# A linear-attention and feed-forward kernel: the second unit's output projection by seven block products, its weight sums in parts and one step sooner

## The chip, the cores and the metric

The kernel runs on one core of a Trainium2 chip. The metric is the device time of one execution in microseconds (us). A core has five engines with queues of their own: TensorE (PE; PEld is its weight load), VectorE (DVE), ScalarE (ACT), GpSimd (POOL) and SyncE (SP, which here only issues transfers). Each engine takes its instructions in the order of its queue; they wait for each other through semaphores.

## The reference

```python
# attention: r, k, v, w of (4, 8, 768, 48), u of (8, 48); state (4, 8, 48, 48) from zero
for t in range(768):
    cur = outer(u * k[t], v[t])
    y[t] = r[t] @ (state + cur)
    state = w[t][:, None] * state + outer(k[t], v[t])
x = y as (3072, 384)             # tokens by heads times head size
h = x @ w_in                     # w_in (384, 2048)
g = h * erf(softplus(h))
out = g @ w_out                  # w_out (2048, 384)
```

All is 32-bit floating point.

## The kernel before

The 3072 tokens are handled in 12 units of 256 tokens (two batches of 128 tokens each, called j). Step s of the kernel does the attention of unit s, and beside it pieces of the feed-forward block of earlier units: the hidden layer of unit s-1 (`hidden`, L1098: six matmuls of 256 columns to a tile `ff`, three to one accumulator half) and the output projection of unit s-3 (`project` or `project_fast`). The order is written out by hand: the attention code calls `place(n)` at eight places of a step (`run(n, ...)` from step 5 on), and a place emits pieces from lists of letters. P is a piece of projection, H a piece of the hidden layer, A the next activation stage of a unit, S1 to S4 are sums of activations, G a sum of weights. The schedule of an engine is the order of emission; nothing reorders it.

Attention. A step splits its 128-token chunks into halves of 64 and combines them by levels 1 to 6. At each level TensorE makes the products (`level_products`, L628), VectorE scales r and k in place for the next level (`scale`, L334; level n+1's products need level n's scaling), and VectorE takes the products of the levels up to 5 under a mask into `own` (`take_level`, L638; ScalarE, L645, takes level 6). From step 5 on, the first levels are done in another way, by rows: VectorE and GpSimd multiply and fade r and k (L456, L463, L485 to L504, L535, L538), VectorE sums the terms (L529), and the sums go out to memory and come back in another order (`by_blocks`, `by_tokens`) to be written into `own` (L590). That work for step s+1 is a generator, `following`, that the step s before it moves on by `next(following)`; each `yield` in `prepare` is where it pauses. In step 4 (`DIRECT`), which makes levels 4 to 6 by itself, it is moved on after level 4, after level 5 and after level 6. The state goes on through `middle` (L1032), a fading on GpSimd (L1018 and L1035) and the state sum (L1036).

Activation. For units 0 to 2, ScalarE makes softplus and erf of half a unit (2048 columns) in `room`, four quarters of 1024 columns, two of them for each half of the unit; VectorE multiplies the result into `h` in two instructions (L1087). `STAGES` and the letter A say how many of these stages are emitted where.

Projection. `project` (L1130) multiplies h by w_out plainly: 32 matmuls of 384 columns for a unit, in two accumulators, and ScalarE copies each out (L1139). `project_fast` (L1213) splits the unit's h in four blocks (a11, a12, a21, a22: by tokens and by halves of the 2048) and w_out in four (b11 to b22), and makes the four output blocks from seven block products of eight matmuls of 192 columns. It needs sums of activations, s1 to s4 (`blend`, L1190 to L1196; s1, s2 and s4 lie in quarters 1, 2 and 3 of `room`, s3 in place of a21), and sums of weights, t1 to t4 (`mix_weights`, L1154; t2, t3 and t4 lie in `mixed`, t1 in place of b12). It uses two accumulators, m0 and m1, which come from the same pool of two buffers as those of the hidden pieces. The sixth and the seventh product are added to the output by VectorE (L1233, L1238), and only then is m0, and m1, free for the next piece. [...]

`SEVEN = 2` says that units 0 and 1 are projected plainly and the others by seven products. Unit 0 is projected in step 3, places 0 to 3; unit 1 in step 4:

```python
order = (
    "A P P P", "A P P P", "A P P H H", "A A S1 S2 G H H s H", "ep H s H m S4 S3 ep H",
)
```

The weight sums t3, t2, t4 are made by VectorE near the end of step 3 (three sums of 1536 columns), t1 by GpSimd in step 4 (G), after the last plain product of unit 1 has read b12. Until the start of step 3, w_out is still being put together from 64-bit words (L261 to L289): its last three pairs of row tiles become ready at places 0 to 2 of step 3.

Of the kernel before, what the change touches and what calls it, by code (L numbers as in the profile page):

```python
# [15 lines left out]
ALU = mybir.AluOpType  # L16

P = 128
FAST = 3
SEVEN = 2  # L20
EP = 64
HC = 64
NC = 2
NJ = 2
FG = 8
# [15 lines left out]
DIRECT = 4  # L41
NEAR_LOG = 4
NEAR = 1 << NEAR_LOG
LOG = 6
# [18 lines left out]
def kernel(  # L63
# [14 lines left out]
    nc = tc.nc  # L78
    PSUM = bass.MemoryType.PSUM

    n_steps, _, _, JP, C = rkw.shape
# [4 lines left out]
    _, NT, DM = w_out.shape  # L86
# [31 lines left out]
    first = const.tile([P, HC], FP32, name="first")  # L118
# [241 lines left out]
    def prepare(s):  # L360
# [185 lines left out]
            add_total(beside, 2)  # L546
        fade(nc.vector, r, 2)
        sum_up(0)
        multiply(nc.vector, 3)
        if levels == NEAR_LOG:  # L550
            fade(beside, k, 3)
# [397 lines left out]
    def attend(s, xT, early, place, behind):  # L949

        c, in_t, vt, made, S, S_next, ends = parts_of(s)
        K = in_t[:, 1]
        RK = by_pair(in_t)


        following = prepare(s + 1) if s + 1 < n_steps else iter(())
        own = made if s >= DIRECT else att.tile([P, NH, HC], FP32, name="own")

        if s == DIRECT:
            next(following)  # L960
        for level in range(near_log(s) + 1 if s == DIRECT else 1, LOG + 1):
            rk = by_pair(made) if level == 1 else RK
            pp = turns.pop("pp", None) or products([P, NE, JP, HC])
            if s == level == 1:
                level_products(pp, rk, level, range(NP))
                turns.pop("hop")()
                level_products(pp, rk, level, range(NP, JP))
                send("br")
            elif s != 2 or level != 2:
                level_products(pp, rk, level)  # L970
            if level == LOG and s == DIRECT:
                spread_blocks(s + 1, pp)
            if s == 1 and 2 < level:
                stages["h"](level + 1)
            scale(s, level)
            if s == 1 and level == 2:
                turns.pop("pending")()
            if s == 1 and level < 3:
                stages["h"](level + 1)
            if s == 1 and level > 1:  # L980
                nc.gpsimd.tensor_copy(out=block_sb[:, 0:1], in_=K[:, 0, 0:1])
                for i in {2: (2, 3)}.get(level, (level + 1,)):
                    stages["o"](i)
            if s != 1:
                early(level - 1)
            got = pp[:].rearrange("p e n t -> p (e n) t")
            if level == 1:
                nc.vector.tensor_mul(
                    own[:], got, first[:, None, :].to_broadcast([P, NH, HC])
                )  # L990
            else:
                take_level(own, pp, level)
            if level > 1 and (s, level) != (1, 4):
                next(following, None)
            if s == 2 and level == 1:

                def ahead():
                    turns["pp"] = products([P, NE, JP, HC])
                    level_products(turns["pp"], RK, 2)

                turns["ahead"] = ahead
            place(level - 1)
            if (s, level) == (1, 4):
                next(following, None)
            if s == 1 and level in (3, 4):
                nc.sync.dma_start(out=loaded[2][0][:, level - 3], in_=rkw[2][:, level - 3])

        from_own(s, own, 1)
        ps = products([P, JP, P])
        for n in range(JP):  # L1010
            nc.tensor.transpose(ps[:, n, :], K[:, n, :], ident[:])  # L1011
        kT = att.tile([P, NH, D], FP32, name="kT", bufs=1)
        nc.scalar.copy(
            kT[:].rearrange("p (e n) d -> p e n d", e=NE),
            ps[:].rearrange("p n (e d) -> p e n d", e=NE)[..., :D],
        )
        if c:
            nc.gpsimd.tensor_mul(  # L1018
                faded[0][:], S[:], ends[:, :, 0:1].to_broadcast([P, JP, D])
            )  # L1020
        next(following, None)
        place(LOG)
        if s == DIRECT - 1:
            for _ in range(3):
                mixing.send(nc.vector)

        ps = products([P, NC, JP, HC])
        ps = [[ps[:, h]] * NE for h in range(NC)]
        state_part(s, kT, ps)
        from_own(s, own, 0)  # L1030
        if c:
            nc.vector.tensor_add(middle[both], faded[0][both], ps[0][0][both, :, :D])  # L1032
        else:
            nc.vector.tensor_copy(middle[both], ps[0][0][both, :, :D])
        nc.gpsimd.tensor_mul(faded[1][:], middle[:], ends[:, :, 1:2].to_broadcast([P, JP, D]))  # L1035
        nc.vector.tensor_add(S_next[both], faded[1][both], ps[1][0][both, :, :D])  # L1036
        for _ in following:
            pass
        place(LOG + 1)
        through_state(s, xT)  # L1040
        behind()
# [102 lines left out]
    def mix_weights():  # L1144

        upper, lower = w_out_sb[:, :FG], w_out_sb[:, FG:]
        b11, b12, b21, b22 = (x[:, :, k * ND : (k + 1) * ND] for x in (upper, lower) for k in range(2))
        t3, t2, t4 = (mixed[:, n] for n in range(3))
        for of, a, op, b in (
            (t3, b22, ALU.subtract, b12), (t2, t3, ALU.add, b11),  # L1150
            (t4, b21, ALU.subtract, t2), (b12, b12, ALU.subtract, b11),
        ):
            engine = yield
            engine.tensor_tensor(out=of, in0=a, in1=b, op=op)  # L1154
        yield

    def half_room(name, shape):
        t = wide.tile(shape, I32, name=name, bufs=3 if name == "words" else 2)
# [232 lines left out]
    def in_order(s, k):  # L1391


        order = (
            "A P P P", "A P P P", "A P P H H", "A A S1 S2 G H H s H", "ep H s H m S4 S3 ep H",
        )
        run_late(s, order[k])

# [12 lines left out]
    def run_late(s, tokens, following=None):  # L1411
# [41 lines left out]
    )  # L1453

    STAGES = {
        1: (0, 0, 0, 0, 0, 0, 1, 0), 2: (1, 0, 0, 0, 0, 0, 2, 1), 3: (1, 1, 1, 0, 0, 2, 1, 1)
    }
    ALONE = {1, 2}

# [11 lines left out]
    for kk in range(KT):  # L1471
        n = D // KT
# [3 lines left out]
    with tc.manual_schedule(  # L1476
# [15 lines left out]
        for s in range(n_steps):  # L1492
            xTs[s] = xs.tile([P, KT, UNIT], FP32, name="xT")
            places = iter(range(8))

            def convert_at(n, late=True):
                if s < len(CONVERT) and n < len(CONVERT[s]):
                    send(CONVERT[s][n][late])

            def place(n):  # L1500
                if n == LOG - 1 and DIRECT - 1 <= s <= DIRECT:
                    load_rows(s + 2)
                for due in {(3, 4): (5,), (4, 3): (6,), (4, 5): (7,)}.get((s, n), ()):
                    load_w(due)
                if s >= DIRECT:
                    in_order(s, next(places))
                    return
                if s in ALONE:
                    if s == 2 and not n:

                        next(hids[0])
                        turns.pop("ahead")()
                    convert_at(n)
                    if (s, n) == (1, LOG - 1):
                        load_w(3)
                        load_v(2)
                    if (s, n) == (2, LOG - 2):
                        load_v(3)
                        nc.sync.dma_start(out=block_sb[:], in_=block_mask)
                        nc.sync.dma_start(out=u_row[:], in_=u_rows)  # L1520
                    if s == 2 and not n:
                        beside(s, next(places))
                        advance(STAGES[s][n])
                        return
                    advance(STAGES[s][n])
                else:
                    advance(STAGES[s][n])
                    convert_at(n)
                    if s == DIRECT - 1 and not n:
                        load_rows(DIRECT)  # L1530
                beside(s, next(places))

            def run(n, following):
                if n == 3 and s < n_steps - 2:
                    load_rows(s + 2)
                if n == 3 and s + 3 < n_steps:
                    load_w(s + 3)
                run_late(s, LATE.get(s, USUAL)[STAGES_LATE.index(n)], following)

            if s > DIRECT:  # L1540
                attend_late(s, run)
                continue
            if s:
                attend(
                    s, xTs[s], lambda n: convert_at(n, False), place, lambda: convert_at(LOG + 2)
                )
            else:
                attend_first(xTs[s])
            if s and s + 2 < n_steps:
                load_step(s + 2)  # L1550
# [109 lines left out]
```

## Time and profile before

| what | value |
|---|---|
| three runs | 579.5, 579.71 and 583.45 us, median 579.71 |
| the profiled execution's own time | 579.58 us |
| its span, first to last instruction | 577.8 us |
| granted TensorE clock | 1.000 |
| busy time: PE, DVE, ACT, POOL | 570.1, 435.1, 355.2, 244.3 us |
| plain projection of one matmul pass, 384 columns (L1130) | 128 passes in 43.2 us, two units |
| block products, 192 columns (L1213, three large groups) | 848 passes in 148.7 us |

Times in the timelines are counted from the start of the span. Step 3 begins with its level-1 products at 91.3, step 4 with its level-4 products at 143.5, step 5 at 192.2, step 6 at 236.5. Busy time of TensorE is a union of pipelined matmuls, so what matters is the distance between the starts of groups. A bracket behind a line of the timeline gives the engine's idle time ahead of it and what ended it.

### The profile page before, as it was taken

How to read it: one execution, taken by the hardware profiler on the slowest of the kernel's cores; microseconds unless marked ns; L12 is line 12 of the kernel's file. 1: busy time of each engine (PE TensorE's matmuls, PEld its weight loads, DVE VectorE, ACT ScalarE, POOL GpSimd, SP SyncE). 2: the span in 40 equal slices, each digit the busy share in tenths (PEclk: the TensorE clock that was granted, in tenths of full speed). 3: DMA queues.
4: the chain of work that ended last, by engine and by line, in shares of the span. 5: the costliest groups of instructions: out<-in, count | busy, mean ns of one | idle time of the engine just before them, and what ended most of it. 6: DMA issues, size and time to landing. Idle time of an engine off the chain costs nothing.

```text
span 577.8 us, 16604 instructions
## 1 busy us (share of the span) xinstructions
PE 570.1 (99%) x7288; PEld 497.2 (86%) x7288; DVE 435.1 (75%) x468; ACT 355.2 (61%) x479; POOL 244.3 (42%) x264
## 2 busy tenths in 40 slices
PE   8999999999999999999999999999999999999997
PEld 6678887688668998998998998898898899988997
DVE  8775876998898899699699599599599527256640
ACT  4658777644448857757756766766766661388700
POOL 4557391604796784284284185175173000000000
PEclk9999999999999999999999999999999999999999
DMA  8595662350444315145245235235232201000000
GB/s 269 185 348 211 237 207 81 147 165 2 145 114 135 109 57 164 36 154 168 36 148 169 40 131 188 39 113 165 44 110 83 47 9 37 0 2 1 28 28 27
DMA packets 54081, 63.24 MB, mean 109 GB/s; under 512 B 35160, under 2 KB 40568, under 8 KB 52984
## 3 DMA queue, kind: packets, MB, share of 16 engines
q1 hardware_dynamic: 53624, 61.98, 33.8%
q8 instruction: 57, 0.93, 0.7%
q10 hardware_dynamic: 384, 0.20, 0.1%
q14 instruction: 16, 0.13, 0.1%
HBM read 52.39 MB, written 8.69 MB: 106 GB/s over the span
## 4 chain that ended last, share of the span: by engine, by line
PE 95%; DMA 2%; ACT 1%; DVE 1%; SPq 0%; issue 0%; DVEq 0%; ACTq 0%
PE m L1098 35%; PE m L1213 32%; PE m L1130 7%; PE pp L628 5%; PE pp L1301 4%; PE y L1301 2%; PE y L660 2%; PE y L686 2%; PE pp L735 2%; DMA words<-in_moe_w_in 1%; PE pp L944 1%; PE pp L1011 1%; DMA u_sb<-in_u 1%; PE pp L1213 0%; PE m L935 0%; SPq L151 0%
## 5 line engine op out<-in xcount | busy, mean ns | idle before, releaser
L1098 PE MATMUL m<-xT,w_in_sb 128*128 128x256 f32 x960 | 215.3, 382 | 0.1
L1098 PEld LDWEIGHTS m<-xT,w_in_sb 128*128 128x128 f32 x960 | 179.7, 190 | 26.2 <-ACT h L1107 1.0
L334 DVE TENSOR_TENSOR in<-in,tot_sb 128x1024 f32<-128x1024 f32 (+1 forms) x55 | 77.4, 1407 | 15.7 <-PE pp L628 14.3
L1107 ACT COPY h<-m 128x512 f32<-128x512 f32 x80 | 46.3, 579 | 51.3 <-PE m L1098 51.1
L1213 PE MATMUL m<-mixed,h 128*128 128x192 f32 x288 | 51.2, 331 | 0.0
L1213 PE MATMUL m<-w_out_sb,h 128*128 128x192 f32 x288 | 50.4, 329 | 0.0
L1213 PEld LDWEIGHTS m<-mixed,h 128*128 128x128 f32 x288 | 46.6, 190 | 1.0
L1213 PEld LDWEIGHTS m<-w_out_sb,h 128*128 128x128 f32 x288 | 46.8, 190 | 0.4
L1213 PE MATMUL m<-w_out_sb,room 128*128 128x192 f32 x272 | 47.1, 326 | 0.0
L1213 PEld LDWEIGHTS m<-w_out_sb,room 128*128 128x128 f32 x272 | 44.6, 190 | 0.3 <-ACT o L1224 0.3
L1058 ACT ACT_TABLE_LOAD x30 | 38.5, 1283 | 8.5 <-DVE h L1063 8.1
L1130 PE MATMUL m<-w_out_sb,h 128*128 128x384 f32 x128 | 43.2, 492 | 0.0
L463 POOL TENSOR_TENSOR words<-words,own 128x384 f32<-128x384 f32 x21 | 31.6, 1502 | 22.8 <-DVE words L494 13.1
L628 PEld LDWEIGHTS pp<-in 48*48 48x48 f32 (+4 forms) x2368 | 30.1, 120 | 12.3 <-issue 7.3
L1054 ACT ACT_TABLE_LOAD x30 | 38.5, 1283 | 2.8 <-issue 2.3
L504 POOL TENSOR_TENSOR words<-words 128x384 f32<-128x384 f32 x28 | 39.7, 1445 | 0.0
L1130 PEld LDWEIGHTS m<-w_out_sb,h 128*128 128x128 f32 x128 | 23.7, 190 | 15.4
L456 POOL TENSOR_TENSOR own<-rest 128x384 f32<-128x384 f32 x7 | 10.0, 1432 | 61.5 <-ACT o L1219 61.5
L628 PE MATMUL pp<-in 48*48 48x32 f32 (+4 forms) x2368 | 33.9, 206 | 1.1 <-DVE in L334 1.1
L504 POOL TENSOR_TENSOR rk<-words 128x384 f32<-128x384 f32 x28 | 32.5, 1190 | 0.0
L529 DVE TENSOR_REDUCE sums<-rk 128x16 f32<-128x768 f32 (+2 forms) x31 | 31.7, 1022 | 0.0
L1054 ACT ACTIVATE room<-h 128x1024 f32<-128x1024 f32 x28 | 29.6, 1059 | 0.3
(204 smaller groups left out, 987.7 us busy)
## 6 DMA issues: line engine op xcount, KB each, us to landing
in<-in_rkw SPq DMA_DIRECT2D x8, 1024.0 KB, 5.0
words<-in_moe_w_in SPq DMA_DIRECT2D x16, 384.0 KB, 5.5
words<-in_moe_w_out SPq DMA_DIRECT2D x16, 384.0 KB, 5.6
words<-in_rk_rows SPq DMA_DIRECT2D x8, 768.0 KB, 5.9
w<-in_rkw SPq DMA_DIRECT2D x11, 512.0 KB, 6.4
v<-in_v SPq DMA_DIRECT2D x12, 384.0 KB, 5.5
out<-o SPq DMA_DIRECT2D x23, 192.0 KB, 3.2
in<-in_rkw SPq DMA_DIRECT2D x7, 512.0 KB, 5.3
```

The costliest lines, as they stand in the source:

```text
L334: nc.vector.tensor_mul(halves, halves, view(tots[level - 1], 0, [[1, n], [2, nb], [0, half]]))
L463: engine.tensor_mul(to, to, of[:, :, None, :].to_broadcast([P, NEAR // 2 // half, half, D]))
L504: engine.tensor_mul(to[:, i], r[:, half:], k[:, part * rows + i, None].to_broadcast([P, half, D]),)
L529: nc.vector.tensor_reduce(out=to, in_=of, axis=mybir.AxisListType.X, op=ALU.add)
L628: nc.tensor.matmul(to, lhsT=rk(1, n)[rows(e), s0 : s0 + m], rhs=right, start=True, stop=True,)
L1054: nc.scalar.activation(sp_room, chunks[0], AF.Softplus)
L1058: nc.scalar.activation(at, sp_room, AF.Erf)
L1098: nc.tensor.matmul(ps[:, ff, :], lhsT=w_in_sb[:, g * FG + f + ff, kk * P : (kk + 1) * P], rhs=xT[:, kk, :], start=kk == 0, stop=kk == KT - 1,)
L1107: nc.scalar.copy(h[:, f : f + FT, :], ps[:])
L1130: nc.tensor.matmul(ps[j][:], lhsT=gs[g][:, f, j * C : (j + 1) * C], rhs=w_out_sb[:, g * FG + f, :], start=g + f == 0, stop=g == NG - 1 and ...
L1213: nc.tensor.matmul(to, lhsT=a[:, f], rhs=b[:, f], start=start and f == 0, stop=f == FG - 1, skip_group_check=True,)
L1301: nc.tensor.matmul(to[:, e], lhsT=a[:, 2 * i + e], rhs=b, start=start and not k, stop=True, skip_group_check=True,)
```

## The change

`SEVEN` becomes 1: unit 1 is projected by seven products too. Its h is summed by `blend` at the end of step 3 and the start of step 4, s1 after `middle`, the other three after the step's last place. For that the gate multiplication of unit 1's second half is emitted ahead of `middle` (`advance(1)`) and no more at the last place of step 3 (`STAGES`).

The weight sums are made in parts: on row tiles 0 to 1 at place 0 of step 3, on 2 to 3 at place 1 (VectorE, three sums of 384 columns each), then t1 on all eight row tiles on GpSimd after level 5 of step 3, behind a one-column copy that reads `own`, and on row tiles 4 to 7 (three sums of 768 columns, VectorE), from the new t1, where all three stood before. G leaves step 4.

In step 4 the activation stages of unit 2 are emitted after the products that read the same quarters of `room`. The generator for step 5 has one more pause, after the sum of its own terms: level 5's scaling and mask copy in step 4 come ahead of the long products (L494) and the third and fourth sum of terms, which then are emitted together after level 5. After level 6 the generator is moved on only behind the place's pieces. All other steps keep their order.

```diff
-SEVEN = 2
+SEVEN = 1
...
         sum_up(0)
+        if s == DIRECT + 1:
+            yield
         multiply(nc.vector, 3)
...
-            if level > 1 and (s, level) != (1, 4):
+            later_on = (s, level) in ((1, 4), (DIRECT, LOG))
+            if level > 1 and not later_on:
+                next(following, None)
+            if (s, level) == (DIRECT, LOG - 1):
                 next(following, None)
...
             place(level - 1)
-            if (s, level) == (1, 4):
+            if later_on:
                 next(following, None)
+            if (s, level) == (DIRECT - 1, LOG - 1):
+                nc.gpsimd.tensor_copy(out=first[:, 0:1], in_=own[:, 0, HC // 4 : HC // 4 + 1])
+                mixing.send(nc.gpsimd)
...
         place(LOG)
         if s == DIRECT - 1:
-            for _ in range(3):
-                mixing.send(nc.vector)
+            advance(1)
...
+        if s == DIRECT - 1:
+            blend(s - 2, 1)
         nc.gpsimd.tensor_mul(faded[1][:], middle[:], ends[:, :, 1:2].to_broadcast([P, JP, D]))
...
-        for of, a, op, b in (
-            (t3, b22, ALU.subtract, b12), (t2, t3, ALU.add, b11),
-            (t4, b21, ALU.subtract, t2), (b12, b12, ALU.subtract, b11),
-        ):
+        first_two = (
+            (t3, b22, ALU.subtract, b12), (t2, t3, ALU.add, b11), (t4, b21, ALU.subtract, t2),
+        )
+        others = (
+            (t2, b22, ALU.subtract, b12), (t3, t2, ALU.subtract, b11), (t4, b21, ALU.subtract, t2),
+        )
+        engine = yield
+        for f in (slice(0, 2), slice(2, 4), slice(4, FG)):
+            for of, a, op, b in others if f.stop == FG else first_two:
+                engine.tensor_tensor(out=of[:, f], in0=a[:, f], in1=b[:, f], op=op)
             engine = yield
-            engine.tensor_tensor(out=of, in0=a, in1=b, op=op)
-        yield
+            if f.stop == FG // 2:
+                engine.tensor_tensor(out=b12, in0=b12, in1=b11, op=ALU.subtract)
+                engine = yield
...
-            "A P P P", "A P P P", "A P P H H", "A A S1 S2 G H H s H", "ep H s H m S4 S3 ep H",
+            "P P P A", "P A P P", "A P H H", "A A S1 S2 H H s H", "ep H s H m S4 S3 ep H",
...
-        1: (0, 0, 0, 0, 0, 0, 1, 0), 2: (1, 0, 0, 0, 0, 0, 2, 1), 3: (1, 1, 1, 0, 0, 2, 1, 1)
+        1: (0, 0, 0, 0, 0, 0, 1, 0), 2: (1, 0, 0, 0, 0, 0, 2, 1), 3: (1, 1, 1, 0, 0, 2, 1, 0)
...
                     advance(STAGES[s][n])
+                    if not n:
+                        mixing.send(nc.vector)
                     convert_at(n)
+                    if n == 1 or n == LOG:
+                        mixing.send(nc.vector)
+                    if n == LOG + 1:
+                        blend(s - 2, 2, 4, 3)
```

## The prediction

> **What bounds the kernel now.** I read the page first (busy times, granted clock, chain by engine), then the chain in order of time, then the timelines of TensorE, VectorE, GpSimd and ScalarE from the third to the fifth step, and the waits of the weight loads.
>
> ```profile
> PE 570.1 (99%) x7288; PEld 497.2 (86%) x7288; DVE 435.1 (75%) x468; ACT 355.2 (61%) x479; POOL 244.3 (42%) x264
> ...
> PEclk9999999999999999999999999999999999999999
> ...
> PE 95%; DMA 2%; ACT 1%; DVE 1%; SPq 0%; issue 0%; DVEq 0%; ACTq 0%
> ```
>
> TensorE is the chain: 99% busy at full clock. Every microsecond taken from its stream is a microsecond of the end, and so is every wait put into it. The chain in order of time prices old and new form of the changed part:
>
> ```profile
> 144.45 7.94 PE m L1130 x24
> 153.24 7.94 PE m L1130 x24
> 162.11 5.36 PE m L1130 x16
> ...
> 193.06 13.42 PE m L1213 x80
> 207.42 5.40 PE m L1213 x32
> ```
>
> The first three lines are unit 1 projected plainly in step 4 (21.24 us); the last two are unit 2 projected by seven products in step 5 (18.82 us).
>
> The timelines of VectorE and GpSimd show where the new work must go. Columns: start, length, engine, line, tiles, count, and the idle time ahead with what ended it.
>
> ```profile
> 102.57 1.34 DVE L638 COPY_PREDICATED own<-mask_sb,pp 128x512 f32<-128x512 int32 x1
> 105.21 1.49 DVE L334 TENSOR_TENSOR in<-in,tot_sb 128x1024 f32<-128x1024 f32 x1 [1.30 <-PE pp L628]
> 109.11 1.83 DVE L456 TENSOR_TENSOR own<-rest 128x384 f32<-128x384 f32 x1
> 121.67 1.22 DVE L334 TENSOR_TENSOR in<-in,tot_sb 128x1024 f32<-128x1024 f32 x1
> 151.96 1.03 DVE L488 TENSOR_TENSOR rk<-words 128x384 f32<-128x384 f32 x2 [2.06 <-POOL words L463]
> 161.90 1.63 DVE L334 TENSOR_TENSOR in<-in,tot_sb 128x1024 f32<-128x1024 f32 x1 [0.31 <-PE pp L628]
> 169.28 3.96 DVE L1087 TENSOR_TENSOR h<-h,room 128x1024 f32<-128x1024 f32 x2
> ```
>
> ```profile
> 102.80 1.83 POOL L289 TENSOR_TENSOR w_out_sb<-w_out_sb,rest 128x768 int32<-128x768 int32 x1 [0.32 <-DVE w_out_sb L281]
> 138.60 5.95 POOL L408 TENSOR_TENSOR tot_sb<-w 128x512 f32<-128x512 f32 x1
> 164.35 7.81 POOL L504 TENSOR_TENSOR words<-words 128x384 f32<-128x384 f32 x4
> 174.86 3.45 POOL L1154 TENSOR_TENSOR w_out_sb<-w_out_sb 128x1536 f32<-128x1536 f32 x1
> ```
>
> The same L334 takes 1.22 us alone and 1.63 beside L504; the pair of L1087 takes 2.35 elsewhere and 3.96 here; L408 on 512 columns takes 1.04 at 104.58 and 5.95 at 138.60. So the two engines wait for each other. Finally the waits of the weight loads around 123 us:
>
> ```profile
> PEld pp L628 <- DVE in L334: 0.3, 1, 0.3
> ```
>
> TensorE's level-6 products start at 122.97, when the L334 that began at 121.67 is done (122.89). VectorE and TensorE are level there: what is late on VectorE in step 3 after 105.21, where its last idle time of the step before 137 lies, is late on TensorE.
>
> **The change part by part**, each cost relative to before.
>
> *Unit 1 by seven products*: 21.24 - 18.82 = 2.42 us off the chain, all on the path: -2.4. Nothing else on TensorE changes. ScalarE gets three copies of output for two, with more than 2 us to spare ahead of the product that waits for each.
>
> *Weight sums by parts.* VectorE's three sums of 1.76 us become nine: twice three on 384 columns (0.55 each, as L463) and three on 768 (0.95 each, as L538). The first three (1.65) fit the idle 1.76 us that ended at 97.70: nothing. The second three follow the L638 that ends at 103.91, ahead of the L334 at 105.21. The 1.30 us of idle time there takes 1.3 of 1.65, so at least 0.35 is late, less 0.27 if that L334 no longer waits behind GpSimd: lower end 0.1 (not below nothing, for VectorE loses no work ahead of 122.89). Upper end: each waits its turn behind GpSimd, which runs L289 to 104.62 and then L408 on 512, 256 and 128 columns (about 0.95, 0.47, 0.25). Sums and GpSimd alternating from 104.55 end L334 at 108.65, not 106.70: 1.95. The L456 row (1.83 for 0.56) shows that such waits happen in this step; the 5.95 of L408 shows VectorE keeping the turn. I take 1.0, between the two.
>
> The Trainium skill's page "SBUF — State Buffer", section "Who interferes with whom", states that a VectorE instruction with two SBUF inputs and a GpSimd instruction that reads SBUF exclude each other, the first to start holding for its whole length. L1087 beside L504 agrees (about 1.98 us each in turn); L408 losing four turns running at 138.60 does not fit a turn for each. By the rule this term would be 1.95 and the sum 1 us higher.
>
> *Step 4's backlog on VectorE.* Leaving out the step 3 term (it moves both engines), I walk the rows. The in-place difference (3.45 on GpSimd) now starts near 123.8, after the level-5 L638 that ends at 123.52, and lasts to 127.2, so the L334 that began at 125.93 waits for it: 1.2 late. The last three sums are 2.9 for 5.3, but the gate product (2.35) moves ahead of `middle`: `middle` ends at 138.8 for 137.6. Then s1 (1.22); GpSimd's fade (0.83) must wait for it, then the state sum (0.55) to 141.3; L334 and L590 (1.22 each) to 143.7; s2, s4, s3 (1.22 each) to 147.3; the L334 of level 4 to 148.5, before 145.74. GpSimd's L408 chain, which at 138.60 waited until VectorE paused, waits for that longer run; its later fade releases L488. I put L488 at 155.2, 3.2 later than 151.96: without GpSimd's delay it would be 152.4, with the full one 156.6. From there to the add of the sixth product: L488 1.03, L463 0.56, L529 0.95, L334 1.3, L638 0.7, L494 2.2, L463 0.56, L529 0.95 and 1.74, add 0.55: 10.5, ending 165.7.
>
> TensorE is ready earlier: 144.38 + 8.0 (three products) + 0.85 + 8.05 + 0.95 (levels 5 and 6, block spread) + 2.7 = 164.9. The next hidden piece needs the accumulator that this add frees: 0.8 us of waiting. The piece after it, 2.65 us on, needs the other, freed by the second add, behind L334 (1.63 to 1.95) and the pair of L1087 (3.96 beside L504): 165.7 + 1.9 + 3.96 + 0.55 = 172.1, against 168.4: 3.7. Together 4.5; with L334 and L1087 at 1.22 and 2.35 it is 2.2. Were VectorE not behind at all, the second add would end at 162.1 + 1.22 + 2.35 + 0.55 = 166.2, ahead of 167.6: nothing, the lower end (no gain, since both adds are new waits). Upper end, with L488 at 156.6: 5.9. I take 4.0, nearer to the contended rows, since L504 runs there.
>
> *Hidden parts.* SP's first store of unit 1 waits for the first add (about 165.7 for 161.7) and holds back the spread of the next step's totals, landed near 169 and first used at 208. The second store is near 172, ahead of the k store at 174.13. The row sums' round trip moves by some 4 us from 182.9; L590 reads it at 186.25 and moves by some 3. Without that cover each would cost its excess, under 1 us. The late step 4 work meets VectorE's 1.79 us of idle ahead of 178.36 and 1.65 ahead of 193.13: I add nothing for step 5.
>
> **Sum**: -2.4 + 1.0 + 4.0 = +2.6 us. The profiled execution is 579.58 us (span 577.8 and 1.8 around it), 0.13 below the median; on the median that is 582.3.
>
> **Rivals.** *The adds come in time, the gain stays (not slower).* The place is the second add of unit 1. If VectorE keeps its turn against GpSimd as at 138.60, L488 is near 152.4 and the pair of L1087 takes 2.35, the add ends before 168 and the stall is under 0.7. With 0.2 in step 3: -2.4 + 0.7 + 0.2 = -1.5, 578.2. The rival decides when the second add ends less than 2 us behind the seventh product. For it: idle time of 0.86, 2.06 and 0.31 us on VectorE in step 4, and level 5's scaling moved ahead of the long products. Against: some 5 us of blends and adds for 3.2 of idle, and the two waits by L504.
>
> *Break even*: stalls of 2 to 3 us in all, 579.7.
>
> *The backlog runs into step 5.* If the upper ends meet (1.95 and 5.9), VectorE is over 5 us late at the row sums, L590 waits for them, and the 1.65 us at 193.13 is used up, so step 5's adds are late too (its hidden products start at 213.61, 0.1 after the add there ends): -2.4 + 1.95 + 5.9 + 1 = +6.5, 586.2. Against it: idle stretches of 2.3 and 2.6 us on VectorE in the steps behind.
>
> *The clock falls in the new gap.* Before, no TensorE gap exceeds 1.1 us and the granted clock is 1.00 throughout. A gap near 3.7 us is new here; a piece of 12 matmuls (2.67 us) at half speed would add 2.7: 585.0. The Trainium skill's page "TensorE: Matmul & The Clock Gate", Part 1, gives about 3.4 us of idle time before the clock halves; no run here shows it.
>
> **How the numbers follow.** Likeliest, stalls larger than the saving: 0.47, own range 580.3 to 584.7. Gain kept 0.28; break even 0.12; into step 5 0.09; clock 0.04. The saving alone gives 577.3, 0.4%, so faster by over 1% (5.8 us, about what a measurement of this kernel can tell) has only an unseen cause: 0.02. Slower by over 1% (above 585.5) takes the last two rivals and a tail: 0.12. Within 1%: 0.86. The range runs from the saving with nothing lost, 577.3, to the backlog case, 586.0.
>
> **What would show it.** Right: seven groups of 16 matmuls near 2.7 us in step 4; the level-6 products of step 3 start 0.5 to 2 us after 122.97; a TensorE gap of 2 to 4 us ahead of the second hidden piece, released by VectorE's second add, and a short one before it; steps of 44.3 us behind. Wrong: step 4's hidden pieces without a gap (then 578), or TensorE gaps beyond step 4.

## The result and the profile after

| | before | after |
|---|---|---|
| median (22 runs each) | 579.25 us | 582.6 us |
| range | 578.12 to 583.45 | 580.32 to 584.14 |
| the profiled execution, its span | 579.58, 577.8 | 581.88, 580.1 |

The ratio is 1.0053, with a 95% interval of 1.0041 to 1.0066: slower by half a per cent, although TensorE has less to do. The page after, to be read beside the one before (lines of kernel.py have moved: L334 stays, L628 is now L630, L1098 L1107, L1213 L1229, L1233 and L1238 L1249 and L1254, L1087 L1096, the weight sums L1167 and L1170):

```profile
PE 569.0 (98%) x7336; PEld 503.6 (87%) x7336; DVE 446.4 (77%) x480; ACT 354.7 (61%) x480; POOL 247.5 (43%) x265
...
PE 66%; DVE 10%; POOL 4%; issue 3%; ACTq 0%; ACT 0%; POOLq 0%; DVEq 0%
```

TensorE was 95% of the chain that ended last; now it is 66%, and VectorE and GpSimd stand in it with 10% and 4%. The waits of the weight loads between 84 and 240 us say where:

```profile
PEld m L1107 <- DVE o L1254: 3.1, 1, 3.1
PEld pp L630 <- DVE in L334: 2.3, 2, 1.4
```

The second was 0.3 before, the first was not there. TensorE's timeline gives both places; of the seven products it shows the first and the last. Each matmul of the code has two records in the profile, so x16 is a product of eight matmuls and x12 a hidden piece of six.

```profile
117.83 0.92 PE L630 MATMUL pp<-in 48*48 48x32 f32 x64 [0.81 <-DVE in L334]
...
124.62 0.76 PE L630 MATMUL pp<-in 48*32 48x32 f32 x64 [0.49 <-DVE in L334]
...
145.10 0.98 PE L630 MATMUL pp<-in 48*56 48x32 f32 x64
146.02 2.87 PE L1229 MATMUL m<-w_out_sb,h 128*128 128x192 f32 x16
...
163.80 2.87 PE L1229 MATMUL m<-w_out_sb,h 128*128 128x192 f32 x16
166.50 2.85 PE L1107 MATMUL m<-xT,w_in_sb 128*128 128x256 f32 x12
172.06 2.86 PE L1107 MATMUL m<-xT,w_in_sb 128*128 128x256 f32 x12 [2.71 <-DVE o L1254]
```

Before, the same two places were:

```profile
143.46 0.98 PE L628 MATMUL pp<-in 48*56 48x32 f32 x64
...
167.30 5.34 PE L1098 MATMUL m<-xT,w_in_sb 128*128 128x256 f32 x24
```

From the level-4 products of step 4 to the first hidden piece it is now 166.50 - 145.10 = 21.40 us, before 167.30 - 143.46 = 23.84: 2.44 saved. But step 3 waits twice ahead of its levels 5 and 6, and step 4 stands still for 2.71 us ahead of the second hidden piece.

To compare kernels I measure between starts of groups on TensorE in the profiled executions: the level-1 products of step 3, level 6 of step 3, level 4 and level 6 of step 4, the transposes (L1011) of step 4, the first products of steps 5 and 6 (step 6's stand at 235.6 before; 236.5 is the projection behind them), the end. What lies ahead of step 3 varied from 90.3 to 93.8 us between the profiles shown here, and is left out.

| kernel | step 3 to its level 6 | level 6 to step 4 | step 4 to its level 6 | to the transposes | to step 5 | step 5 | to the end | sum |
|---|---|---|---|---|---|---|---|---|
| before | 31.71 | 20.49 | 17.64 | 12.07 | 19.01 | 43.44 | 342.18 | 486.53 |
| after | 33.25 | 20.49 | 17.76 | 12.58 | 19.01 | 43.45 | 342.18 | 488.71 |
| second add first | 32.73 | 20.49 | 17.76 | 9.60 | 19.01 | 45.60 | 342.17 | 487.36 |
| sums late | 31.71 | 20.49 | 17.76 | 14.69 | 19.01 | 43.45 | 342.54 | 489.65 |
| both | 31.71 | 20.54 | 17.80 | 10.28 | 19.01 | 45.59 | 342.18 | 487.10 |
| sums in parts alone | 33.94 | 20.49 | 17.64 | 12.07 | 19.01 | 43.43 | 342.17 | 488.75 |

The difference of 2.18 us lies in steps 3 and 4 alone: 1.54 in step 3, and in step 4 the saving of 2.44 less a stall of 3.07 (17.76 + 12.58 for 17.64 + 12.07). The medians are 3.35 apart; a good part of the rest is the clock, below.

### The profile page after: what moved, and what is told of

Same layout as the page of the kernel before. It is cut to its first block, busy times and chain, and to the rows that moved or that the text cites. A ratio compares the mean times of both kernels' runs of the same rounds, so it can differ in the third digit from the quotient of the medians.

```text
span 580.1 us, 16713 instructions
## 1 busy us (share of the span) xinstructions
PE 569.0 (98%) x7336; PEld 503.6 (87%) x7336; DVE 446.4 (77%) x480; ACT 354.7 (61%) x480; POOL 247.5 (43%) x265
## 4 chain that ended last, share of the span: by engine, by line
PE 66%; DVE 10%; POOL 4%; issue 3%; ACTq 0%; ACT 0%; POOLq 0%; DVEq 0%
PE m L1229 28%; PE m L1107 25%; PE pp L1317 4%; PE y L1317 2%; PE y L662 2%; PE pp L630 2%; POOL tot_sb L408 2%; DVE in L334 2%; PE y L688 1%; DVE sums L529 1%; PE pp L737 1%; DVE words L494 1%; DVE words L463 1%; DVE own L640 1%; DVE h L1096 1%
## 5 line engine op out<-in xcount | busy, mean ns | idle before, releaser
L1107 PE MATMUL m<-xT,w_in_sb 128*128 128x256 f32 x960 | 215.6, 382 | 3.2 <-DVE o L1254 2.7
L1107 PEld LDWEIGHTS m<-xT,w_in_sb 128*128 128x128 f32 x960 | 179.6, 190 | 29.6 <-DVE o L1254 3.1
L334 DVE TENSOR_TENSOR in<-in,tot_sb 128x1024 f32<-128x1024 f32 (+1 forms) x55 | 81.0, 1474 | 12.8 <-PE pp L630 11.5
L1116 ACT COPY h<-m 128x512 f32<-128x512 f32 x80 | 46.2, 579 | 53.3 <-PE m L1107 53.2
L1229 PE MATMUL m<-mixed,h 128*128 128x192 f32 x320 | 56.7, 331 | 0.0
L1229 PE MATMUL m<-w_out_sb,h 128*128 128x192 f32 x320 | 56.1, 329 | 0.0
L1229 PEld LDWEIGHTS m<-mixed,h 128*128 128x128 f32 x320 | 51.8, 190 | 1.0
L1229 PE MATMUL m<-w_out_sb,room 128*128 128x192 f32 x304 | 52.5, 326 | 0.0
L1229 PEld LDWEIGHTS m<-w_out_sb,h 128*128 128x128 f32 x320 | 52.0, 190 | 0.5
L1229 PEld LDWEIGHTS m<-w_out_sb,room 128*128 128x128 f32 x304 | 49.9, 190 | 0.0
L630 PEld LDWEIGHTS pp<-in 48*48 48x48 f32 (+4 forms) x2368 | 30.1, 120 | 12.5 <-DVE in L334 4.6
L630 PE MATMUL pp<-in 48*48 48x32 f32 (+4 forms) x2368 | 33.9, 206 | 1.7 <-DVE in L334 1.7
L408 POOL TENSOR_TENSOR tot_sb<-tot_sb 128x256 f32<-128x256 f32 (+4 forms) x50 | 28.4, 567 | 3.8
L1063 ACT ACTIVATE room<-h 128x1024 f32<-128x1024 f32 x28 | 29.6, 1057 | 0.3
L1187 ACT COPY y<-h 128x1024 f32<-128x1024 f32 x12 | 12.2, 1017 | 26.7 <-DVE h L1072 17.0
```

Of the source, the lines that this page charges most:

```text
L334: nc.vector.tensor_mul(halves, halves, view(tots[level - 1], 0, [[1, n], [2, nb], [0, half]]))
L408: nc.gpsimd.tensor_mul(new, pair[:, :, 0], pair[:, :, 1])
L630: nc.tensor.matmul(to, lhsT=rk(1, n)[rows(e), s0 : s0 + m], rhs=right, start=True, stop=True,)
L1063: nc.scalar.activation(sp_room, chunks[0], AF.Softplus)
L1107: nc.tensor.matmul(ps[:, ff, :], lhsT=w_in_sb[:, g * FG + f + ff, kk * P : (kk + 1) * P], rhs=xT[:, kk, :], start=kk == 0, stop=kk == KT - 1,)
L1116: nc.scalar.copy(h[:, f : f + FT, :], ps[:])
```

## The experiments

The kernels ran in three sets, each on one chip beside the kernel before, whose median there was 579.50, 579.67 and 580.25 us.

### The second add first

```diff
-"P P P A", "P A P P", "A P H H", ...
+"P P P A", "P A P P", "P A H H", ...
```

> The changed kernel with the letters of the third place in step 4 as "P A H H": unit 1's second output add stands ahead of the gate product of unit 2 on VectorE. Theory A (the gap ahead of the second hidden piece is the queue order on VectorE: scaling, pair of gate products, then the add): the add ends near 168.2 instead of 172.0, the 2.71 us gap is gone; but VectorE has as much to do as before and has no idle time from there to step 5, so some of it (up to 1.4 us, after 1.65 us of idle time at 195.4 is used up) comes back ahead of the first hidden piece of step 5. Span 578.4 to 577.4 against 580.1. Rival B (all of the stretch is bound by VectorE and the wait only moves): span 580.0, a gap of over 2.5 us at another place. Rival C (only the order): 577.0 and no gap in step 5. If the lower clock in some runs comes from the gap, all runs have clock 1.000 here.

Ratio to before 1.0031 (1.0016 to 1.0046). The gap in step 4 is gone: level 6 to the transposes takes 9.60 us, 2.98 less. Two gaps came up in step 5:

```profile
202.62 2.87 PE L1229 MATMUL m<-w_out_sb,room 128*128 128x192 f32 x16 [0.91 <-ACT o L1240]
...
213.80 2.43 PE L1107 MATMUL m<-xT,w_in_sb 128*128 128x256 f32 x10 [1.11 <-DVE o L1249]
```

Step 5 takes 45.60 for 43.45. So the queue order makes the gap at its place (theory A), and 2.15 of the 2.98 us come back; A had said up to 1.4. The rows of VectorE and ScalarE say why (the first is the changed kernel, the other two this one):

```profile
189.66 1.22 DVE L1072 TENSOR_TENSOR h<-h,pp 128x1024 f32<-128x1024 f32 x1
...
188.39 1.21 DVE L1072 TENSOR_TENSOR h<-h,pp 128x1024 f32<-128x1024 f32 x1
...
189.68 1.28 ACT L1067 ACT_TABLE_LOAD   x1 [2.03 <-DVE h L1072]
```

VectorE reaches L1072, ahead of step 5, 44.5 us after the start of step 4 in both kernels (189.66 - 145.10, 188.39 - 143.86): the moved add gives TensorE time and VectorE none. ScalarE now waits 2.03 us for L1072, and the copy L1240, for which TensorE waits 0.91, stands behind that in its queue. One of 12 runs had a mean clock of 0.996, not none.

### The weight sums late

```diff
-for f in (slice(0, 2), slice(2, 4), slice(4, FG)):
+for f in (slice(0, 2), slice(2, FG)):
...
-                    if n == 1 or n == LOG:
+                    if n == LOG:
```

with t1 made behind the first part.

> The changed kernel with the weight sums of row tiles 2 and 3 made at the end of step 3 with those of 4 to 7 (three sums of 1152 columns, some 1.35 us each) instead of at place 1. Theory A (step 3's term is the three sums ahead of the scaling): the two gaps of 0.81 and 0.49 us in step 3 are gone and level 6 starts near 123.1, not 124.6; VectorE's end of step 3 is only 0.3 earlier, the second add of unit 1 stays within 0.5 us of 172.0, so the gap there grows by about 1.2 and the span is 579.6 to 579.9. Rival B (the two terms just add): gap in step 4 unchanged at 2.7, span 578.6.

Step 3 is back to 31.71, so the three sums at place 1 are its whole term. The gap in step 4 did not grow (2.70 us), with a wait of 0.32 more ahead of the first hidden piece: on this point rival B is nearer. Counted from the start of step 3, the second hidden piece starts 1.04 us earlier (79.65 for 80.69), where TensorE had gained 1.54. Yet the ratio is 1.0050 (1.0033 to 1.0067). The profile of this run shows why: columns of the second view are the stretch, its length, busy time of PE, PEld, DVE, ACT and POOL, the granted clock, the DMA share, GB/s.

```profile
170.90 4.36 PE L1107 MATMUL m<-xT,w_in_sb 128*128 128x256 f32 x12 [2.70 <-DVE o L1254]
```

```profile
164.00:168.10 4.10, 3.78 (x19) 2.92 (x17) 4.10 (x4) 2.78 (x2) 4.10 (x4) 1.00 0.16 54
...
171.00:175.00 4.00, 4.00 (x12) 2.96 (x12) 3.93 (x3) 0.00 (x0) 4.00 (x3) 0.64 1.00 282
175.00:180.00 5.00, 5.00 (x56) 4.39 (x56) 4.50 (x3) 3.52 (x4) 3.83 (x4) 0.95 0.64 250
```

Behind the gap the same 12 matmuls take 4.36 us for 2.86, at a granted clock of 0.64. That is some 4 x 0.36 + 5 x 0.05 = 1.7 us lost, and 1.7/580 is the 0.3% by which the mean clock of such a run is under 1: 0.997, in five of six runs here.

### The gap filled, in the changed kernel and with late sums

```diff
-"A P H H"
+"A P H W H"       # W: five matmuls of ident by ident, 256 columns, into the free product bank
```

> The changed kernel with five matmuls of the identity (256 columns, into a free bank, some 2.2 us together) on TensorE between the two hidden pieces in step 4, where the gap of 2.71 us is. Theory A (the runs at a mean granted clock of 0.997, 12 of 22 of the changed kernel, are those in which the gap lowers the clock for a few us): no run at 0.997, span of the profiled run unchanged at 580.1 within 0.3, and the median 0.7 to 1 us lower than that of the changed kernel, near 581.7. Rival B (the lower clock has another cause, as the start of the program): half of the runs stay at 0.997 and the median at 582.6.

> The weight sums of row tiles 2 and 3 late, as alone before, and the five identity matmuls in the gap of step 4. The late sums alone had a mean granted clock of 0.997 in five of six runs and 0.64 in the 4 us behind the gap in the profile. Theory A (the gap makes the clock fall): no run at 0.997 from that place, clock 1.00 behind the gap in the profile, and the part from level 6 of step 4 to the transposes behind the hidden pieces 12.6 to 12.9 us, not 14.69. Rival B (clock falls for another reason): 0.997 in most runs again.

One of six and one of nine runs had a clock under 0.998, for 12 of 22 in the changed kernel and five of six with late sums. In the first profile the one drop stands at 37 to 50 us (0.87), far from step 4, which had 1.00, but it too stands behind a TensorE gap, of 1.54 us (the second view has the columns explained above):

```profile
40.46 1.03 PE L630 MATMUL pp<-in 48*56 48x32 f32 x64 [1.54 <-DVE in L334]
41.42 4.54 PE L1107 MATMUL m<-xT,w_in_sb 128*128 128x256 f32 x12
```

```profile
43.00:45.00 2.00, 2.00 (x6) 1.64 (x5) 2.00 (x3) 1.62 (x2) 1.33 (x2) 0.50 1.02 405
```

The kernel before has 1.13 us at that place, at full clock; it is its widest gap between matmuls. In the second profile the clock is 1.00 through step 4, and level 6 to the transposes takes 13.24 us against 14.69 without the fill (A had said 12.6 to 12.9; a wait of 0.49 ahead of the first hidden piece is in it). So the gap lets the clock fall. The times did not follow: medians 582.69 and 582.85, ratios 1.0063 (1.0049 to 1.0077) and 1.0047 (1.0028 to 1.0065). From step 3 on, the filled kernel takes 488.68 us at full clock, as the changed one does (488.71). Why its five runs at full clock are about 1 us longer than those of the changed kernel stays open: so few runs, with a start that varies, do not settle it. With late sums and the fill, 0.6 us of the time lies outside the span: it exceeds the span by 2.4 us on average (1.75 to 2.90 in the nine runs), by 1.8 in every other kernel here; the cause of that is open too.

### The sums in parts alone

The kernel before, with t3, t2, t4 made in three parts at place 0, at place 1 and at the end of step 3; t1 stays in step 4, unit 1 plain.

> The kernel before with one part of the change alone: the sums t3, t2, t4 in parts (row tiles 0 to 1 at place 0 and 2 to 3 at place 1 of step 3, 4 to 7 at the end of step 3); unit 1 is still projected plainly. Theory A (the parts at place 1 make VectorE late, and TensorE's products of levels 5 and 6 wait): level 6 in step 3 starts 1.4 to 1.7 us after 122.97 and nothing makes it good: span 579.3 against 577.8. Rival B (the step 3 delay comes from the rest of the change, as the in-place difference or the blends): span within 0.3 of 577.8.

```profile
118.01 0.92 PE L628 MATMUL pp<-in 48*48 48x32 f32 x64 [1.44 <-DVE in L334]
...
124.80 0.76 PE L628 MATMUL pp<-in 48*32 48x32 f32 x64 [0.49 <-DVE in L334]
```

Ratio 1.0028 (1.0016 to 1.0039), 488.75 us from step 3 on: 2.22 more than before, from step 3 alone (33.94 for 31.71). Theory A, with 0.5 us more than it said. Where the rest of the change hid 0.7 us of this, and what part of it is not the sums, is read from the rows below.

### No blends

> The changed kernel without the four sums of unit 1's activations (they are left out; its products read what lies in their place, so four instructions of 1.22 us are gone from VectorE around the start of step 4, all else stands). Theory A (the gap in step 4 is the sum of a backlog on VectorE, of which the blends are the largest part, and the queue order): the second add of unit 1 ends 2.5 to 4 us earlier than 172.0 against the start of step 4, and the gap of 2.71 us shrinks to at most 0.5. Rival B (the order and GpSimd's long products alone make the gap): it stays over 1.5.

```profile
162.53 0.55 DVE L1249 TENSOR_TENSOR o<-o,m 128x384 f32<-128x384 f32 x1 [0.88 <-issue]
...
169.07 0.54 DVE L1254 TENSOR_TENSOR o<-o,m 128x384 f32<-128x384 f32 x1
```

```profile
169.66 2.86 PE L1107 MATMUL m<-xT,w_in_sb 128*128 128x256 f32 x12 [0.90 <-DVE o L1254]
```

This is one run. Against the start of step 4, the second add ends 1.9 us earlier (169.61 - 144.60 = 25.01, after 172.01 - 145.10 = 26.91). Neither theory's number: the four sums make 1.8 of the 2.7 us, and the remaining 0.9 is the scaling (2.09) and the pair of gate products (3.96) in front of the add, with no backlog at all: VectorE stood idle for 0.88 us ahead of the first add there.

### Both edits, and step 5's order

```diff
+ DIRECT + 1: ("s P", "m", "ey P m P s P ep P", "P m k22y P F k11p F F", ...)   # in LATE, second kernel only
```

> Both edits: the second output add ahead of the gate product in step 4, and the weight sums of row tiles 2 and 3 at the end of step 3. Theory A (VectorE has no spare time from step 3 into step 5, so what TensorE no longer waits in steps 3 and 4 comes back in part in step 5): no gap over 0.4 us in steps 3 and 4; step 5, which took 43.45 us from its first to the next step's first products and 45.60 with the add moved alone, takes 46.0 to 47.2; from the start of step 3 to the end 486.6 to 487.6 us against 486.53 before and 488.71 with the change. Rival B (the gains add): step 5 at 45.6 or less, 485.8 or less. Clock 1.000 in step 4 in all runs.

> Both edits, and step 5's order changed too: on ScalarE the third product's copy ahead of a softplus, on VectorE the sixth product's add ahead of a gate product and the seventh's ahead of a scaling. Theory A (step 5's gaps are waits for these copies and adds in their queues, and VectorE gets later idle time of 2.4 us in step 5): step 5 takes 43.5 to 44.6 us, the whole from step 3 on 485.0 to 485.9, so 0.6 to 1.5 us under the kernel before. Rival B (VectorE lacks the time itself): step 5 stays over 45.5 and the gap stands at another instruction.

Both edits: ratio 1.0003 (0.9987 to 1.0020), no change from before. Step 3 is whole again, step 4 shorter than before, and step 5 at 45.59 as with the add alone: the step 3 part adds (rival B there), but 0.68 came up in step 4 again (a gap of 0.50, A had said none over 0.4), and the sum of 487.10 lies where A put it. One of 12 runs had a mean clock of 0.997; where it fell is not on record. With step 5 reordered, the gap ahead of the fifth product is gone, and stands elsewhere:

```profile
214.56 8.04 PE L1107 MATMUL m<-xT,w_in_sb 128*128 128x256 f32 x36 [1.15 <-DVE o L1249]
223.84 1.35 PE L1107 MATMUL m<-xT,w_in_sb 128*128 128x256 f32 x5 [1.25 <-ACT h L1116]
```

Step 5 takes 45.86, ratio 1.0017 (1.0003 to 1.0032). My theory of the orders failed here; rival B holds. The second of these gaps is VectorE's too: ScalarE's L1116 stood behind a copy (L1187) that had waited 4.02 us for VectorE's L1206.

### The row sum and the last long products behind the adds

```diff
-            if (s, level) == (DIRECT, LOG - 1):
-                next(following, None)
...
             if later_on:
                 next(following, None)
+                if s == DIRECT:
+                    next(following, None)
```

in the changed kernel, with both edits, and with late sums alone.

> The changed kernel with the row sum of 1.74 us on 1536 columns (the second of two, ahead of unit 1's first output add in step 4) and GpSimd's last four long products, which wait for it, moved behind the second output add. Theory A (queue order and the port: the adds wait for that sum, and the gate products take 2.0 us each only while GpSimd's long products run): first add 1.6 to 1.7 us earlier, one gate product at 1.22, second add near 169.5 against 172.0, gap 0.1 to 0.5 us for 2.71, level 6 to transposes 10.0 to 10.4 for 12.58 us; VectorE's work is the same and GpSimd's products end no earlier, so step 5 takes 43.5 to 45. Rival B (GpSimd's products contend just the same): gap over 0.9.

> The kernel with both edits (second add first, weight sums late), which equalled the kernel before (1.0003), with that row sum and GpSimd's last four long products behind the adds. Theory A (VectorE and GpSimd have no spare time up to step 5, so moving work inside the stretch gives nothing): step 5 stays at 45.0 to 46, from step 3 on 486.3 to 487.2, no faster than before. Rival B (less waiting between VectorE and GpSimd gives VectorE time back): step 5 under 44.6 and the whole under 485.8, some 0.2% faster than before.

> Weight sums late, and the row sum with the last four long products behind the second output add, with the gate product where the change has it. Theory A: as the gap of step 4 was 2.70 with the late sums alone, it is 0.1 to 0.6 here, no clock of 0.997 from that place, step 3 to its level 6 in 31.71; what comes back in step 5 is under 1 us, as the gate product is not late: from step 3 on 485.0 to 486.2, equal to 0.3% faster than before. Rival B (all saved comes back in step 5): 486.5 to 487.2.

```profile
170.96 0.54 DVE L1254 TENSOR_TENSOR o<-o,m 128x384 f32<-128x384 f32 x1
...
171.56 2.86 PE L1107 MATMUL m<-xT,w_in_sb 128*128 128x256 f32 x12 [1.87 <-DVE o L1254]
216.21 9.02 PE L1107 MATMUL m<-xT,w_in_sb 128*128 128x256 f32 x40 [0.99 <-DVE o L1249]
```

In the first, the second add ends only 0.94 us earlier against the start of step 4: the pair of gate products took 3.95 us again, beside GpSimd's first four long products, which also took longer (6.80 us for 5.83). The gap fell to 1.87, so rival B holds, and 0.99 came back in step 5: 488.62 from step 3 on, as with the change. Ratio 1.0029 (1.0013 to 1.0044).

With both edits: 487.33, ratio 1.0005 (0.9988 to 1.0021), so nothing is gained, as theory A said. Step 5 takes 46.60, longer than either theory had it, with a gap of 1.89 us behind which the clock fell:

```profile
206.00:211.00 5.00, 5.00 (x84) 4.68 (x83) 4.90 (x6) 1.16 (x1) 3.74 (x5) 0.68 0.01 3
```

With late sums neither theory holds: the gap is 2.36 us, where I had it at 0.1 to 0.6, and nothing came back in step 5 (43.45). The clock fell behind the gap, and nine of 12 runs had a mean clock under 0.998; 488.41 and 1.0023 (1.0003 to 1.0043).

```profile
171.00:175.00 4.00, 4.00 (x30) 2.79 (x32) 3.93 (x4) 0.19 (x1) 3.09 (x2) 0.57 0.72 206
```

No version beat the kernel before; the two with both edits equal it. VectorE's rows show what the orders have in common. Here is the instruction ahead of step 5, L1072, in the kernel before (L1063 there), with both edits, and with the row sum behind in the changed kernel; those of the changed kernel (189.66) and of the second add first (188.39) stand above:

```profile
187.39 1.22 DVE L1063 TENSOR_TENSOR h<-h,pp 128x1024 f32<-128x1024 f32 x1
188.24 1.21 DVE L1072 TENSOR_TENSOR h<-h,pp 128x1024 f32<-128x1024 f32 x1
190.76 1.22 DVE L1072 TENSOR_TENSOR h<-h,pp 128x1024 f32<-128x1024 f32 x1
```

From the start of step 3 VectorE needs 96.13 us to it before, 98.29 with the change, 97.75 with the second add first, 97.49 with both edits and 98.95 with the row sum behind. Against before, these last three are 1.62, 1.36 and 2.82 us late there; in each, TensorE waits about 1 us for VectorE ahead of the first hidden piece of step 5, and the time lost from step 3 on (0.83, 0.57 and 2.09) is that lateness less 0.7 to 0.8. So in them VectorE's work sets the time, and moving TensorE's waits about does not shorten that work.

## Why the prediction was right, and where it was off

The forecast was 582.3 us, slower within 1%, by stalls larger than the saving; that is what happened, at the two places named. That the median of 582.6 lies so near is in part luck: the 2.6 us were added to 579.71, the median of three runs, where 22 runs give 579.25; the measured difference is 3.35 us, and the sum's errors partly cancel. Term by term:

*Seven products*: -2.4 forecast, -2.44 measured.

*Step 3*: 1.0 forecast, between 0.1 and 1.95; 1.54 measured. The rows of VectorE after, and GpSimd beside it:

```profile
102.99 1.35 DVE L640 COPY_PREDICATED own<-mask_sb,pp 128x512 f32<-128x512 int32 x1
104.14 1.32 DVE L1167 TENSOR_TENSOR mixed<-w_out_sb 128x384 f32<-128x384 f32 x1
105.50 1.28 DVE L1167 TENSOR_TENSOR mixed<-mixed,w_out_sb 128x384 f32<-128x384 f32 x1
106.81 0.85 DVE L1167 TENSOR_TENSOR mixed<-w_out_sb,mixed 128x384 f32<-128x384 f32 x1
107.59 1.42 DVE L334 TENSOR_TENSOR in<-in,tot_sb 128x1024 f32<-128x1024 f32 x1
```

```profile
103.22 1.83 POOL L289 TENSOR_TENSOR w_out_sb<-w_out_sb,rest 128x768 int32<-128x768 int32 x1 [0.32 <-DVE w_out_sb L281]
105.01 1.35 POOL L408 TENSOR_TENSOR tot_sb<-w 128x512 f32<-128x512 f32 x1
```

Sums that took 0.55 to 0.56 us at place 0, with GpSimd idle, take 1.32, 1.28 and 0.85 here: the alternation of the upper bound. L334 ends at 109.00 for 106.70, or 2.2 later once the 0.1 by which step 3 began later is taken off. Some 0.65 of this is made good by the L535 behind it: 0.95 us, before 1.58, since GpSimd's fade that blocked it now stands behind t1. The bounds had not seen that gain.

Another 0.31 is not the sums. The first L276 of step 3 waits for ScalarE, whose row came later against the start of step 3 (before, then after):

```profile
97.70 0.97 DVE L276 TENSOR_SCALAR y<-y 128x768 int32<-128x768 int32 x1 [1.76 <-ACT y L261]
...
98.12 0.97 DVE L276 TENSOR_SCALAR y<-y 128x768 int32<-128x768 int32 x1 [0.42 <-ACT y L261]
```

This L276 begins 6.44 us after the start of step 3 before, 6.75 with the change, 6.81 with the sums alone, and 6.24 with the second add first, whose step 3 is that of the change and whose term is yet 1.02. With late sums it begins at 7.12 and costs nothing (31.71); ahead of the sums at place 1 it adds to them. If it does so in full, the term without it is 1.23 and 1.22 in the two kernels with the whole change, and 1.86 with the sums alone, close under the upper bound of 1.95. So the alternation came almost in full, and the 1.0 taken between the bounds was near because of a gain that it did not foresee: luck.

The rule of the Trainium skill's page "SBUF — State Buffer", section "Who interferes with whom", gave 1.95; these rows bear it out for sums and scaling. L408 on 512 columns took 4.81 us at 142.69, over several VectorE instructions, so a turn for each is not what every row shows.

*Step 4*: 4.0 forecast (nothing to 5.9), 3.07 measured. The walk, with 1.64 us added for the later start of step 4, against the rows:

| point | walk | measured |
|---|---|---|
| L488 begins | 156.8 | 156.82 |
| first add ends | 167.3 | 166.45 |
| first hidden piece could begin | 166.5 | 166.50 |
| second add ends | 173.7 | 172.01 |

```profile
156.82 1.03 DVE L488 TENSOR_TENSOR rk<-words 128x384 f32<-128x384 f32 x2 [1.38 <-POOL words L463]
...
165.90 0.55 DVE L1249 TENSOR_TENSOR o<-o,m 128x384 f32<-128x384 f32 x1
166.36 1.31 DVE L334 TENSOR_TENSOR in<-in,tot_sb 128x1024 f32<-128x1024 f32 x1
167.59 3.96 DVE L1096 TENSOR_TENSOR h<-h,room 128x1024 f32<-128x1024 f32 x2
171.47 0.54 DVE L1254 TENSOR_TENSOR o<-o,m 128x384 f32<-128x384 f32 x1
```

The pair of gate products has the 3.96 that was taken from before. The terms that were sized too long are the stretch from L488 to the first add (10.5, measured 9.6: the rows I added overlap by 0.1 each, and L494 took 1.83 for 2.2) and the scaling (1.9, measured 1.31). So the 0.8 us ahead of the first hidden piece did not appear, and 3.7 became 2.7.

*No cost in step 5*: right (43.45 for 43.44), but because TensorE was late too: VectorE stood 2.16 us late ahead of step 5 (98.29 for 96.13), and TensorE as much. As soon as step 4 no longer waited, step 5 was 2.1 us longer.

*The clock*: what the sum left out. It was a rival at 0.04, priced at 2.7 us on top; the late sums' profile shows 1.7. Of 22 runs of the changed kernel, 12 have a mean clock of 0.997; they average 583.28 us, the other ten 581.72. So the clock falls in about every second run, at 1.56 us, some 0.85 on average. Of 73 runs of the kernel before in the three sets, four had a mean clock under 0.998, all in the third set (four of 29). The forecast's sum without the clock was 0.4 too long (2.6 for 2.18), and this and the 0.85 left out cancel in part. That the clock of the changed kernel itself falls behind its gap is inferred from the kernels with late sums, whose gap is the same or nearly so and whose profiles show it; its own profile was one at full clock.

The Trainium skill's page "TensorE: Matmul & The Clock Gate", Part 1, puts the fall after about 3.4 us without activity. Here it came behind TensorE gaps of 2.70, 2.36, 1.89 and 1.54 us, and in part of the runs alone; the measurement decides.

## What to carry to other kernels

Fewer matmuls on the bounding engine are worth their time only if the engine that feeds it can keep up: here 2.4 us saved on TensorE were paid with sums and adds on a VectorE that had some 3 us of idle time in step 4, and moving the waits about gave back the loss but no gain. Walk the feeding engine's queue from row to row with the durations that it has beside its neighbour (2.0 us for a gate product, not 1.2), and look at what stands ahead of the instruction that frees a buffer. A gap of some 2 us in TensorE cost its length here and, in part of the runs, the slower clock behind it.

## What the runs showed of the hardware

Behind a TensorE gap of 1.5 to 2.7 us the granted clock can fall. Four profiles show it, at 0.50 to 0.68 for 2 to 5 us, behind gaps of 1.54, 1.89, 2.36 and 2.70 us; a hidden piece that takes 2.86 us at full clock took 4.36 to 4.54 there. It is not bound to happen: the profile of the changed kernel has a gap of 2.71 us at full clock. A mean clock under 0.998 was found in 12 of 22 runs with that gap, five of six with 2.70 and nine of 12 with 2.36; in one of six and one of nine when five idle matmuls shortened the gap to 0.55; in one of 12 with gaps of 1.87 and 0.99, and three of 12 with 1.89, beside four of 29 of the kernel before on the same chip. In most of these runs the place of the fall is not on record.

VectorE's sums of two operands and GpSimd's work prolong each other: three sums on 384 columns took 1.32, 1.28 and 0.85 us beside GpSimd, and 0.55 to 0.56 with GpSimd idle.
